# Decoding weights in a three-layer kernel: the sign bit through a parametric ReLU, and earlier decoding for the second layer

## The chip, the cores and the metric

The kernel runs on one core of a Trainium2 chip. The metric is the device time of one launch in microseconds, as the median of several runs. The core has a matrix engine (TensorE; PE in the profile, its weight loads PEld), VectorE (DVE), ScalarE (ACT), GpSimd (POOL) and SyncE (SP), whose queue issues all DMAs here. The engines work side by side and wait for each other through semaphores.

## The reference

Attention for 4 batches, 8 heads, 576 tokens of 64 values, half of the heads with a local mask and half with a strided one; then a gated layer and a softplus layer over the 2304 tokens. Cut to what matters:

```
attn = softmax(where(mask, q @ k.T / 8, -1e9)) @ v
x = attn as 2304 tokens x 512
xn = x / sqrt(mean(x * x) + 1e-6) * rms_g
g = xn @ w_gate;  x = (g / (1 + exp(-g))) * (xn @ w_val) @ w_out      # layer 1, 1536 wide
h = x @ w_in;  out = (max(h, 0) + log1p(exp(-|h|))) @ w_out2          # layer 2, 2048 wide
```

The weights arrive as 64-bit floating point numbers. The kernel reads their bits and makes 32-bit ones of them itself.

## The kernel before

All matrix products of the two layers are done in three matmuls of reduced 32-bit precision (L459): each operand is split into a high part (`ob`, `tb`, `win`, `wout`, `gh`, written by ACT) and a rest (written by DVE or POOL with a subtraction, L376 or L377 through `two`).

The 2304 tokens stand in five chunks of 512 (the last has 256). Layer 1 works on them in two passes. The first pass (chunks 0 and 1) runs while attention for the later batches is still computed, so PE has products of layer 1 (L459) between the small matmuls of attention (L604, L617, L706, L760). At its end the square sums of the last chunks are turned into factors (`stats`, L490 to L493), the chunks are scaled, and `combine` and `build` make the sums of a Strassen product (`tb`): the change of passes. The second pass (chunks 2 to 4) takes the 12 column blocks of layer 1 in a loop with the counter `s`; `quad` does the Strassen product of a block, and `chain1` silu and gate (L972, L974, L975). Then layer 2 goes over the chunks in the same two groups, with `chain2` for softplus.

`decode` (L384) makes one 128 x 512 tile of 32-bit weights. A 512 KB load brings the 64-bit words into one of two buffers `raw`. ACT scales the upper words, read as 32-bit numbers, by 2 to the power -112, which puts sign, exponent and mantissa where three left shifts bring them to their place (L392, into the tile `t`: `w`, `cvt` or `cvtx`). The three low bits of the mantissa come from the lower words into `cvu`: by ACT from a 16-bit view (L393) or by DVE with a shift to the right (L395). A left shift of `t` would push out the sign, so DVE first joins the sign to the low bits (L397) and then shifts `t` and joins both (L400). There are 74 decoded tiles: 42 of layer 1, of which six are decoded twice over the two passes (blocks 0 and 1), and 32 of layer 2. Layer 2's tiles are decoded ahead by `early2`, written back to memory (`w_kept`, L404) and fetched later (L407): 24 of them in the loop of the second pass, 8 in the first four steps of layer 2.

The order of all instructions is set by a planner (`Program`, `Trial`): it gets each instruction with an estimated length and its reads and writes, and lays out each engine's list by due times. Instructions with an `alt` may go to another engine: evictions of attention (`evict`, L291, L292 or L294) and the low bits to ACT or DVE, subtractions and sums (`two`) to DVE or POOL. A small change in `decode` thus moves instructions everywhere. Tables of activation functions are loaded by `table` (L304).

Of the kernel before, what the change touches and what calls it, by code (L numbers as in the profile page):

```python
# [10 lines left out]
F32 = mybir.dt.float32  # L11
F32R = mybir.dt.float32r
U16 = mybir.dt.uint16
U32 = mybir.dt.uint32
# [3 lines left out]
ALU = mybir.AluOpType  # L18
# [241 lines left out]
def attn_glu_softplus(  # L260
# [17 lines left out]
    def all_of(key):  # L278
        return (key, 0, 1 << 30)
# [20 lines left out]
    def dma(kb, fn, r, w):  # L300
        pr.add("SP", 650, fn, r, w, kb=kb)

    def table(name):
        pr.add("ACT", 1300, lambda: nc.scalar.preload_act_table_set(name), [], [all_of("table")])  # L304

    class Ring:
        def __init__(self, tiles, name, first=0):
# [76 lines left out]
    def decode(src, t, kt, keep):  # L384

        raw, kraw = raws.next()
        u, ku = cvu.next()
        words = raw.bitcast(U32).rearrange("p (n two) -> p n two", two=2)
        wlo, whi = words[:, :, 0], words[:, :, 1]
        quarters = raw.bitcast(U16).rearrange("p (n four) -> p n four", four=4)  # L390
        dma(340, lambda: nc.sync.dma_start(out=raw, in_=src), hold, [kraw])
        act(512, lambda: nc.scalar.activation(t, whi.bitcast(F32), AF.Copy, scale=2.0 ** -112), [kraw], [kt])  # L392
        pr.add("ACT", 180 + 512 / 0.98, lambda: nc.scalar.activation(  # L393
            u, quarters[:, :, 1], AF.Identity, bias=low, scale=2.0 ** -13), [kraw, all_of("eps")], [ku], alt=(68 + 512 / 1.5,
            lambda: nc.vector.tensor_scalar(out=u, in0=wlo, scalar1=29, scalar2=None,  # L395
                                            op0=ALU.logical_shift_right)))
        dve(560, lambda: nc.vector.scalar_tensor_tensor(  # L397
            out=u, in0=t.bitcast(U32), scalar=0x80000000, in1=u, op0=ALU.bitwise_and, op1=ALU.bitwise_or),
            [kt, ku], [ku])
        dve(560, lambda: nc.vector.scalar_tensor_tensor(  # L400
            out=t.bitcast(U32), in0=t.bitcast(U32), scalar=3, in1=u,
            op0=ALU.logical_shift_left, op1=ALU.bitwise_or), [kt, ku], [kt])
        if keep >= 3 * AGAIN:
            dma(170, lambda: nc.sync.dma_start(out=wk[keep], in_=t), [kt], [("wk", keep, keep + 1)])  # L404

# [683 lines left out]
    with tc.manual_schedule():  # L1089
# [141 lines left out]
        for s, f in enumerate([*range(AGAIN, W1N), *range(AGAIN)]):  # L1231
            prep1(f, 1)
            w = w_at(f, 1)
            c0, c1, c4 = SIDES[1]
            odd = []

            def gap(k):
                if 0 < k < 3:
                    odd.append(plain(w, k - 1, c4, o_banks))
                if k == 2:  # L1240
                    g[f, c4] = chain1(*odd, 256, True)
                if k and (s < W1N - 1 or len(todo) > 4):
                    drain(2 if f % 2 else 1)

            (gb0, vb0), (gb1, vb1) = quad(w, gap)
            g[f, c0] = chain1(gb0, vb0)
            g[f, c1] = chain1(gb1, vb1)
            for k in range(max(0, 3 * s - 6), min(3 * s - 3, 2 * W1N)):
                early2(k)
            drain(max(0, len(todo) - 6))  # L1250
            if f % 2:
                drain(len(todo))
                todo.extend(outs1(f, s == 1, (c0, c1, c4)))
        drain(len(todo))
        table("softplus")
        for side, (c0, c1, c4) in enumerate(SIDES):
# [2 lines left out]
            n2 = W2N // 2  # L1259
            for p in range(n2):  # L1260
                i = prep2(p, c4 is not None, "POOL" if p == 0 or side == 0 and p < 4 else "DVE")
                if side == 0 and p < 4:
                    early2(2 * W1N + 2 * p)
                    early2(2 * W1N + 2 * p + 1)
                def gap(k):
                    if c4 is not None and 0 < k < 3:
                        g[2 * p + k - 1, c4] = chain2(plain(i, k - 1, c4, o_banks), 256, True)
# [86 lines left out]
```

## Time and profile before

| | us |
|---|---|
| median of 3 runs | 892.98 |
| lowest, highest | 891.08, 894.34 |
| span of the profiled execution | 893.0 |
| PE busy in it | 877.7 |
| DVE busy | 716.4 |
| ACT busy | 509.1 |
| POOL busy | 66.2 |

The profiled execution's own time is its span, 893.0 us, from the first to the last instruction. PE's matmuls are pipelined: one of 512 columns is shown with about 0.39 us, and the next begins 0.23 us later, so a PE that is shown as busy may still lose a little. The clock granted to PE is shown as 1.00 of its full speed in nearly all of the span. Attention and the first pass of layer 1 reach to some 245 us, the change of passes to some 288, the second pass to some 515, layer 2 to the end.

### The profile page before, as it was taken

To read this page: it belongs to the slowest core of one execution; us is meant where nothing else is said; L and a number is where in the kernel's file an instruction comes from. 1 tells how busy PE (TensorE), PEld (TensorE's weight loads), DVE (VectorE), ACT (ScalarE), POOL (GpSimd) and SP (SyncE) were. 2 spreads that over 40 slices of the span, in tenths; PEclk is the share of its full clock that TensorE was granted. 3 is DMA by queue.
4 is the path that set the end of the run, shared out by engine and by line. 5 is a ranking of instruction groups with operands and counts; after the bars stand their busy time and mean duration, and the time that the engine had idled before them with its cause. 6 is when DMAs were issued, how large, how long until landed. Compare 5 with 4: busy or idle time off the path is not lost.

```text
span 893.0 us, 14103 instructions
## 1 busy us (share of the span) xinstructions
PE 877.7 (98%) x5372; PEld 726.9 (81%) x5372; DVE 716.4 (80%) x1316; ACT 509.1 (57%) x977; POOL 66.2 (7%) x60
## 2 busy tenths in 40 slices
PE   7999999999999999999999999999999999999998
PEld 6677877888877888888888888888888888888887
DVE  4999999997699986888889798877798466666645
ACT  3997766663454677564656478544474655434331
POOL 1010202110012001010100020000000000000000
PEclk8999999999999999999999999999999999999999
DMA  7755766532211256454542035311114011111003
GB/s 251 251 194 167 252 219 205 171 97 102 74 56 48 84 167 206 150 178 151 167 138 88 19 105 191 130 47 48 48 48 165 24 48 48 48 29 43 0 1 118
DMA packets 41140, 102.17 MB, mean 114 GB/s; under 512 B 4720, under 2 KB 5744, under 8 KB 41072
## 3 DMA queue, kind: packets, MB, share of 16 engines
q1 hardware_dynamic: 41072, 101.27, 35.1%
q8 instruction: 42, 0.69, 0.3%
q14 instruction: 26, 0.21, 0.1%
HBM read 80.28 MB, written 20.97 MB: 113 GB/s over the span
## 4 chain that ended last, share of the span: by engine, by line
PE 89%; DVE 6%; ACT 2%; DMA 1%; issue 1%; SPq 0%; DVEq 0%
PE bank L459 85%; PE bank L760 1%; DVE xs L1008 1%; PE bank L706 1%; PE bank L617 1%; DMA id_sb<-ident 1%; DVE tb L376 1%; DVE xs L376 1%; DVE gv L376 0%; PE bank L483 0%; ACT eb L664 0%; PE bank L604 0%; ACT eb L668 0%; DVE gv L492 0%; DVE w L376 0%
## 5 line engine op out<-in xcount | busy, mean ns | idle before, releaser
L459 PE MATMUL bank<-ob,win 128*128 128x512 f32 (+1 forms) x1560 | 438.8, 361 | 2.0 <-DVE xs L1008 0.7
L459 PEld LDWEIGHTS bank<-ob,win 128*128 128x128 f32 x1560 | 282.8, 188 | 55.8 <-issue 2.3
L459 PE MATMUL bank<-tb,win 128*128 128x512 f32 x672 | 232.5, 392 | 0.0
L459 PEld LDWEIGHTS bank<-tb,win 128*128 128x128 f32 x672 | 125.0, 188 | 22.9 <-ACT ssq L919 0.2
L1030 DVE TENSOR_TENSOR xs<-bank,xs 128x512 f32<-128x512 f32 (+1 forms) x127 | 87.1, 687 | 43.4 <-PE bank L459 41.7
L430 ACT ACTIVATE win<-w 128x512 fp32r<-128x512 f32 (+1 forms) x136 | 83.1, 615 | 49.2 <-PE bank L459 22.6
L459 PE MATMUL bank<-wout,ghx 128*128 128x512 f32 x304 | 99.9, 389 | 0.0
L459 PE MATMUL bank<-wout,gh 128*128 128x512 f32 (+1 forms) x276 | 90.3, 386 | 0.0
L376 DVE TENSOR_TENSOR win<-w,win 128x512 fp32r<-128x512 f32 (+1 forms) x121 | 82.3, 683 | 7.9 <-ACT win L430 5.2
L459 PE MATMUL bank<-ghx,wout 128*128 128x512 f32 x224 | 83.4, 392 | 0.0
L459 PE MATMUL bank<-gh,wout 128*128 128x512 f32 (+1 forms) x256 | 79.5, 352 | 1.0 <-DVE xs L1008 1.0
L1008 DVE TENSOR_TENSOR xs<-bank,xs 128x512 f32<-128x512 f32 (+1 forms) x100 | 62.6, 634 | 14.0 <-PE bank L459 12.6
L459 PEld LDWEIGHTS bank<-wout,ghx 128*128 128x128 f32 x304 | 56.9, 188 | 11.9
L459 PEld LDWEIGHTS bank<-wout,gh 128*128 128x128 f32 x276 | 51.3, 188 | 10.5
L459 PE MATMUL bank<-wout,glx 128*128 128x512 f32 x152 | 53.5, 389 | 0.0
L923 DVE TENSOR_TENSOR gv<-bank,gv 128x512 f32<-128x512 f32 x48 | 33.1, 690 | 24.4 <-PE bank L459 14.1
L459 PEld LDWEIGHTS bank<-gh,wout 128*128 128x128 f32 x256 | 45.2, 189 | 9.1 <-DVE xs L1008 1.9
L459 PEld LDWEIGHTS bank<-ghx,wout 128*128 128x128 f32 x224 | 42.0, 188 | 8.5
L459 PE MATMUL bank<-wout,gl 128*128 128x512 f32 (+1 forms) x138 | 48.0, 386 | 0.0
L376 DVE TENSOR_TENSOR w<-w 128x256 f32<-128x256 f32 x108 | 46.5, 430 | 0.9
L919 ACT ACTIVATE gv<-bank 128x512 f32<-128x512 f32 x48 | 28.6, 597 | 31.9 <-PE bank L459 31.4
L459 PE MATMUL bank<-glx,wout 128*128 128x512 f32 x112 | 43.3, 395 | 0.2 <-DVE glx L376 0.2
(162 smaller groups left out, 1276.4 us busy)
## 6 DMA issues: line engine op xcount, KB each, us to landing
raw<-w SPq DMA_DIRECT2D x74, 512.0 KB, 3.8
w<-w_kept SPq DMA_DIRECT2D x52, 256.0 KB, 2.6
qk<-qk SPq DMA_DIRECT2D x15, 608.0 KB, 6.7
w_kept<-cvtx SPq DMA_DIRECT2D x25, 256.0 KB, 2.8
cvt<-w_kept SPq DMA_DIRECT2D x25, 256.0 KB, 2.7
w_kept<-w SPq DMA_DIRECT2D x20, 256.0 KB, 2.7
w_kept<-cvt SPq DMA_DIRECT2D x17, 256.0 KB, 2.0
cvtx<-w_kept SPq DMA_DIRECT2D x17, 256.0 KB, 2.7
```

The source lines that it names most:

```text
L376: pr.add("DVE", 68 + n / 0.96, lambda: getattr(nc.vector, name)(o, x, y), r, w, alt=(110 + n * 2.3, lambda: getattr(nc.gpsimd, name)(o, x, ...
L430: act(n, lambda: nc.scalar.activation(h, t, AF.Copy), [kt], [reg(0, o + lo, o + hi)])
L459: lambda a=a, b=b, i=i, st=st, mv=mv: nc.tensor.matmul(o, lhsT=st[a], rhs=mv[b], start=(first and i == 0), stop=(last and i == m - 1), ski ...
L617: nc.tensor.matmul(sp[o, a * nk:(a + 1) * nk], lhsT=qt[r, c:c + 64], rhs=qt[r, QW + c:QW + c + nk], start=False, stop=True, skip_group_che ...
L706: pr.add("PE", 108, lambda a=a, a0=a0, tp=tp: nc.tensor.transpose(tp[:kp, a * 128:a * 128 + 128], pv[:, a0 + a, :], id_sb), [kpv, all_of(" ...
L760: pr.add("PE", 59 if loc else 36, lambda a=a, h=h, o=o, t=t: nc.tensor.matmul(xb[64 * h:64 * h + 64, a * nq:(a + 1) * nq], lhsT=vt[r0:r1, ...
L919: act(CH, lambda: nc.scalar.activation(o, y[0], AF.Copy), [y[1]], [ko])
L923: dve(CH, lambda: nc.vector.tensor_add(o[0], y[0], o[0]), [y[1], o[1]], [o[1]])
L1008: dve(n, lambda: nc.vector.tensor_add(x, pb, x), [kp, kx], [kx])
L1030: dve(n, lambda x=x, pb=pb: nc.vector.tensor_add(x, pb, x), [kp, kx], [kx])
```

## The change

In `decode` ACT's scaling becomes a parametric ReLU: positive numbers are scaled as before, negative ones are also multiplied by -2 to the power 32. Their result is positive and has bit 28 set, which the left shift by three brings to the sign's place. The instruction that joined the sign goes. What is left is one shift and one join. Where ACT makes the low bits, DVE shifts `t` and joins them as before. Where DVE takes that step (`shift`), it now shifts `t` into `cvu`, and the join reads the lower words of `raw` itself and shifts them to the right. Both forms of the second step now wait for the first; the join now also reads `raw`. The table for softplus waits for the last parametric ReLU (`slope`). In the loop of the second pass three tiles of layer 2 a step are decoded from the second step on, all 32 of them, and layer 2 decodes none.

```diff
-        pr.add("ACT", 1300, lambda: nc.scalar.preload_act_table_set(name), [], [all_of("table")])
+        pr.add("ACT", 1300, lambda: nc.scalar.preload_act_table_set(name), [], [all_of("table")] + [all_of("slope")] * (name == "softplus"))
...
+        ti = t.bitcast(U32)
         dma(340, lambda: nc.sync.dma_start(out=raw, in_=src), hold, [kraw])
-        act(512, lambda: nc.scalar.activation(t, whi.bitcast(F32), AF.Copy, scale=2.0 ** -112), [kraw], [kt])
+        act(512, lambda: nc.scalar.activation(t, whi.bitcast(F32), AF.Prelu, scale=2.0 ** -112, alpha=-2.0 ** 32),
+            [kraw, all_of("slope")], [kt])
+        shifted = []
+
+        def shift():
+            shifted.append(nc.vector.tensor_scalar(out=u, in0=ti, scalar1=3, scalar2=None, op0=ALU.logical_shift_left))
+
+        def join():
+            a, b, n, op = (wlo, u, 29, ALU.logical_shift_right) if shifted else (ti, u, 3, ALU.logical_shift_left)
+            nc.vector.scalar_tensor_tensor(out=ti, in0=a, scalar=n, in1=b, op0=op, op1=ALU.bitwise_or)
+
         pr.add("ACT", 180 + 512 / 0.98, lambda: nc.scalar.activation(
-            u, quarters[:, :, 1], AF.Identity, bias=low, scale=2.0 ** -13), [kraw, all_of("eps")], [ku], alt=(68 + 512 / 1.5,
-            lambda: nc.vector.tensor_scalar(out=u, in0=wlo, scalar1=29, scalar2=None,
-                                            op0=ALU.logical_shift_right)))
-        dve(560, lambda: nc.vector.scalar_tensor_tensor(
-            out=u, in0=t.bitcast(U32), scalar=0x80000000, in1=u, op0=ALU.bitwise_and, op1=ALU.bitwise_or),
-            [kt, ku], [ku])
-        dve(560, lambda: nc.vector.scalar_tensor_tensor(
-            out=t.bitcast(U32), in0=t.bitcast(U32), scalar=3, in1=u,
-            op0=ALU.logical_shift_left, op1=ALU.bitwise_or), [kt, ku], [kt])
+            u, quarters[:, :, 1], AF.Identity, bias=low, scale=2.0 ** -13), [kraw, kt, all_of("eps")], [ku],
+            alt=(68 + 512 / 1.92, shift))
+        dve(560, join, [kraw, kt, ku], [kt])
...
-            for k in range(max(0, 3 * s - 6), min(3 * s - 3, 2 * W1N)):
+            for k in range(max(0, 3 * s - 3), min(3 * s, 2 * W2N)):
                 early2(k)
...
-                if side == 0 and p < 4:
-                    early2(2 * W1N + 2 * p)
-                    early2(2 * W1N + 2 * p + 1)
```

The code behind `decode` stands five lines lower in the changed kernel (L459 becomes L464). The planner's lists change in many places. Three of them follow.

PE in the front, the last part before layer 1 and attention run without gaps. `bank_72` and `bank_71` with `ob,win` are the 12 and 12 products of block 1 with chunk 0; `L706` (`L711` after) are transposes of attention, `L760` (`L765`) its products with v. Before:

```order
L706 MATMUL bank_73<-id_sb,eb_120 96x128 x3
L706 MATMUL bank_74<-id_sb,eb_120 96x128
L459 MATMUL bank_72<-ob,win_90 128x512 x9
L760 MATMUL bank_75<-pt_124,xs 64x64 x6
L760 MATMUL bank_75<-pt_125,xs 64x64 x2
L459 MATMUL bank_72<-ob,win_90 128x512 x3
L706 MATMUL bank_73<-id_sb,pp_123 128x128 x3
L706 MATMUL bank_74<-id_sb,pp_123 128x128 x3
L459 MATMUL bank_71<-ob,win_90 128x512 x2
L760 MATMUL bank_76<-pt_126,vb_114 64x54 x3
```

After:

```order
L464 MATMUL bank_72<-ob,win_90 128x512 x3
L711 MATMUL bank_73<-id_sb,eb_120 96x128 x3
L711 MATMUL bank_74<-id_sb,eb_120 96x128
L464 MATMUL bank_72<-ob,win_90 128x512 x9
L765 MATMUL bank_75<-pt_124,xs 64x64 x6
L765 MATMUL bank_75<-pt_125,xs 64x64 x2
L464 MATMUL bank_71<-ob,win_90 128x512 x9
L711 MATMUL bank_73<-id_sb,pp_123 128x128 x3
L711 MATMUL bank_74<-id_sb,pp_123 128x128 x3
L464 MATMUL bank_71<-ob,win_90 128x512 x3
L765 MATMUL bank_76<-pt_126,vb_114 64x54 x3
```

All 24 products now stand ahead of that `L765`, 14 did before; the other ten stood behind it and its neighbours.

DVE in the same place, up to the first instruction of the gate (`L972`, `L977` after). `mz` and `pp` belong to attention's softmax. Before:

```order
L397 SCALAR_TENSOR_TENSOR cvu_82<-w_83,cvu_82 128x512
L679 TENSOR_SCALAR mz_133<-mz_133 128x5
L376 TENSOR_TENSOR pp_123<-eb_121,mz_132 128x6x54
L680 RECIPROCAL mz_133<-mz_133 128x5
L400 SCALAR_TENSOR_TENSOR w_83<-w_83,cvu_82 128x512
L376 TENSOR_TENSOR pp_123<-eb_117,mz_133 128x5x54
L493 SCALAR_TENSOR_TENSOR ssq<-gv_84,ssq 128x512
L395 TENSOR_SCALAR cvu_82<-raw_80 128x512
L972 TENSOR_TENSOR gv_85<-bank_77,ssq 128x512
```

After:

```order
L402 SCALAR_TENSOR_TENSOR cvtx<-raw_80,cvu_82 128x512
L376 TENSOR_TENSOR pp_123<-eb_121,mz_132 128x6x54
L683 TENSOR_REDUCE mz_133<-eb_117 128x5
L291 COPY xs<-bank_75 128x128
L684 TENSOR_SCALAR mz_133<-mz_133 128x5
L292 TENSOR_SCALAR xs<-bank_75,rg_sb 128x128
L685 RECIPROCAL mz_133<-mz_133 128x5
L498 SCALAR_TENSOR_TENSOR ssq<-gv_84,ssq 128x512
L376 TENSOR_TENSOR pp_123<-eb_117,mz_133 128x5x54
L977 TENSOR_TENSOR gv_85<-bank_77,ssq 128x512
```

The tile `w` of block 1 is now joined further ahead, the next tile (`cvtx`) stands where its join stood, and evictions (`xs<-bank`) stand between. From the same instruction at 24.91 us to the first `L975` (`L980`), DVE has 91 instructions before and 96 after.

POOL in the change of passes. Before:

```order
L377 TENSOR_TENSOR xs<-xs,ssq_b 128x512
L377 TENSOR_TENSOR win_90<-w_83,win_90 128x512
L377 TENSOR_TENSOR ob<-xs,ob 128x512
L377 TENSOR_TENSOR w_83<-w_83 128x256
L377 TENSOR_TENSOR win_90<-w_83,win_90 128x512
L377 TENSOR_TENSOR ob<-xs,ob 128x256
L377 TENSOR_TENSOR tb<-xs,tb 128x512
L377 TENSOR_TENSOR xs<-xs,ssq 128x512
```

After:

```order
L377 TENSOR_TENSOR xs<-xs 128x512
L377 TENSOR_TENSOR wout_99<-cvtx,wout_99 128x512
L377 TENSOR_TENSOR win_90<-w_83,win_90 128x512
L377 TENSOR_TENSOR ob<-xs,ob 128x512
L377 TENSOR_TENSOR tb<-xs,tb 128x512
L377 TENSOR_TENSOR xs<-xs,ssq 128x512
```

Eight become six; in the same place (from the first `ssq_b` of the statistics to the first sum of the Strassen product) DVE's 68 become 70.

## Rows read from the trace of the kernel before

**Rows 1.** The page's first part: busy us, share of span, instructions.

```profile
PE 877.7 (98%) x5372; PEld 726.9 (81%) x5372; DVE 716.4 (80%) x1316; ACT 509.1 (57%) x977; POOL 66.2 (7%) x60
```

**Rows 2.** The chain in order of time: start us, us, what.

```profile
284.96 105.70 PE bank L459 x552
...
525.82 362.90 PE bank L459 x1687
```

**Rows 3.** Stretches: length; busy PE, PEld, DVE, ACT, POOL; PE clock; DMA share; GB/s.

```profile
24.91:60.37 35.46, 31.85 (x466) 23.39 (x467) 33.58 (x92) 32.74 (x109) 4.25 (x6) 1.00 0.73 235
60.15:243.12 182.97, 182.48 (x1416) 146.54 (x1417) 160.14 (x306) 115.95 (x207) 23.28 (x21) 1.00 0.50 159
246.30:288.49 42.19, 40.26 (x178) 32.12 (x177) 42.01 (x69) 21.86 (x38) 10.43 (x8) 1.00 0.16 49
285.00:511.00 226.00, 225.97 (x1177) 193.27 (x1178) 194.30 (x348) 137.93 (x243) 15.77 (x13) 1.00 0.41 133
```

**Rows 4.** Groups by line: busy us, mean ns; idle before, and what ended it.

```profile
L393 ACT ACTIVATE cvu<-raw,low 128x512 uint32<-128x512 uint16 x44 | 33.6, 764 | 15.0 <-DVE cvtx L400 8.1 <-DVE w L400 4.6 <-DVE cvt L400 1.5
...
L397 DVE SCALAR_TENSOR_TENSOR cvu<-w,cvu 128x512 uint32<-128x512 uint32 x28 | 19.2, 685 | 3.3 <-ACT cvu L393 1.8 <-ACT w L392 1.4
...
L392 ACT ACTIVATE w<-raw 128x512 f32<-128x512 f32 x28 | 18.5, 672 | 7.1 <-DMA raw<-w 3.4 <-DVE mz L632 2.9 <-DVE win L376 0.6
```

**Rows 5.** Stretches, L397 alone: length, DVE busy (count), clock, DMA share, GB/s.

```profile
25.00:62.00 37.00, 4.09 (x6) 1.00 0.73 233
62.00:245.00 183.00, 19.86 (x29) 1.00 0.50 158
285.00:525.00 240.00, 21.79 (x30) 1.00 0.38 126
525.00:893.00 368.00, 5.51 (x8) 1.00 0.21 69
```

**Rows 6.** DVE in order of time, front: start us, us, instruction, idle before.

```profile
21.48 0.49 DVE L291 COPY pt<-bank 128x324 f32<-128x324 f32 x1
21.89 0.42 DVE L291 COPY xs<-bank 128x256 f32<-128x256 f32 x1
...
50.41 0.35 DVE L292 TENSOR_SCALAR xs<-bank,rg_sb 128x72 f32<-128x72 f32 x1 [0.33 <-ACT xs L294]
...
57.50 0.42 DVE L395 TENSOR_SCALAR cvu<-raw 128x512 uint32<-128x512 uint32 x1
57.84 0.68 DVE L972 TENSOR_TENSOR gv<-bank,ssq 128x512 f32<-128x512 f32 x1
...
59.77 0.68 DVE L397 SCALAR_TENSOR_TENSOR cvu<-cvtx,cvu 128x512 uint32<-128x512 uint32 x1
60.37 0.69 DVE L975 TENSOR_TENSOR gv<-bank,gv 128x512 f32<-128x512 f32 x1
```

**Rows 7.** The page's DMA issues: count, size of one, us from issue to landing.

```profile
raw<-w SPq DMA_DIRECT2D x74, 512.0 KB, 3.8
```

**Rows 8.** PE in order of time, end of the front.

```profile
60.08 2.79 PE L459 MATMUL bank<-ob,win 128*128 128x512 f32 x11
62.86 0.73 PE L459 MATMUL bank<-gh,wout 128*128 128x512 f32 x2
```

**Rows 9.** POOL and DVE in order of time, change of passes.

```profile
249.08 1.41 POOL L377 TENSOR_TENSOR xs<-xs,ssq_b 128x512 f32<-128x512 f32 x1 [56.48 <-DVE ssq_b L493]
...
249.85 2.89 DVE L376 TENSOR_TENSOR xs<-xs,ssq_b 128x512 f32<-128x512 f32 x2
```

**Rows 10.** Waits of PE, 236 to 290 us: total us, times, longest.

```profile
PE bank L459 <- DVE xs L1008: 1.7, 3, 0.7
```

**Rows 11.** Groups by line: the loads of activation tables.

```profile
L304 ACT ACT_TABLE_LOAD x13 | 16.7, 1283 | 0.9 <-PEq L1342 0.7
```

## The prediction

> **What bounds the kernel now.** I read the page's busy times first, then the chain of work in order of time, then the busy time by stretch, then the waits of the stretches in which PE is not full. PE is busy for 98% of the span, DVE for 80%, ACT for 57% [rows 1]. The chain says what that means: from 284.96 us on it is PE for 105.70 us, and from 525.82 us for 362.90 us, with nothing between PE's instructions [rows 2]. By stretch PE is busy for 182.48 of 182.97 us in the second part of attention and 225.97 of 226.00 us in the second pass of layer 1 [rows 3]. There an instruction less on DVE shortens nothing. Two stretches are left. In the front, 24.91 to 60.37 us, PE is busy for only 31.85 of 35.46 us, while DVE is at 33.58 and ACT at 32.74 us: both feed PE late. In the change of passes, 246.30 to 288.49 us, PE has 40.26 of 42.19 us and DVE 42.01 [rows 3]. The whole visible idle time is 3.6 us in the one and 1.9 us in the other, and the change has to earn its gain there.
>
> **Part 1, one DVE instruction a tile less.** The joining of the sign (L397) goes for all 74 tiles: 6, 29, 30 and 8 in the four stretches shown, one more between them [rows 5]. It lasts 685 ns [rows 4], but the next DVE instruction starts 0.60 us after it (59.77 to 60.37) [rows 6], so DVE gives back 74 x 0.60 = 44 us. Of these, 29 x 0.60 = 17 us (part of attention) and 38 x 0.60 = 23 us (layers 1 and 2) lie beside a full PE and are worth nothing. Six, 3.6 us, lie in the front.
>
> **Part 2, what replaces it.** On ACT a Copy with a scale becomes a parametric ReLU with a scale. The trace has no such instruction. Below, its bound is the Copy's 672 ns; above, the Identity with a pointer bias, 764 ns [rows 4]. I take the Copy, since both slopes are constants in the instruction; the upper end would cost ACT 6 x 0.09 = 0.5 us in the front. The three low bits still come from ACT (46 tiles, 44 before) or, in 28 tiles, from DVE as a shift of one source; the shift before it kept DVE for 0.34 us (57.50 to 57.84) [rows 6] and the new one does the same on unstrided data, so I cost that edit at nothing. New are two waits. The low bits now wait for the first pass over the tile. On ACT that is the instruction just ahead in its own queue; on DVE it delays what is queued behind by at most the Copy's 0.67 us, where the order has put other work between. And in the DVE form the raw words are held until the join, some 0.34 + 0.60 us longer plus what stands between, about 1.5 us. What covers this is that two raw buffers alternate and a load lands in 3.8 us [rows 7], while tiles come 183 / 29 = 6.3 to 240 / 30 = 8 us apart [rows 5]; if that cover were gone a tile would come 1.5 us late.
>
> **Part 3, the eight tiles that move.** They leave layer 2 (526 us on, 8 of the L397 [rows 5]) for the second pass of layer 1. With them go eight loads and eight stores on SP's queue, eight to sixteen ACT instructions and eight to sixteen on DVE, ahead of other work there. DVE loses 30 x 0.60 = 18 us in that pass and takes at most 8 x (0.60 + 0.34) = 7.5 us; ACT rises from 137.9 by at most 8 x (0.67 + 0.76) = 11.4 us of 226; the DMA engines are at 0.41 [rows 3]. So PE hides it on both sides, and I cost it at nothing. The softplus table now waits for the last of them, decoded in the last round of a loop in which PE is full. If that cover were gone, softplus would start later by one load and one decode, 3.8 + 0.67 + 0.94 = 5.4 us.
>
> **Part 4, the new order in the front.** The planner spends the 3.6 us. Up to the first gate product (L975, at 60.37 us before), DVE has 96 instructions instead of 91: six sign joins less, one final join more, one split of `win` less (it goes to POOL), and in their place eleven evictions of attention from ACT, one `ob` and one `pp`. At the rows' pitch (0.41 us for the largest eviction, 21.48 to 21.89 [rows 6]; 0.20 to 0.41 for the rest) that is -3.6 + 0.6 - 0.6 + 4.25 = +0.65 us. ACT's own list to the first silu comes out even. PE, in the order, does all 24 products of the first half ahead of the place where it did 14 before. Ten matmuls at 0.25 us (60.08 to 62.86 us for 11 [rows 8]) look like 2.5 us won. They aren't: before, these ten and one more ran from 60.08 to 62.86 us and covered the wait for `gh`, which PE read at once when it came [rows 8]. After the change PE reaches the same `gh` with the same 49 products behind it, and the end is set by when DVE and ACT deliver `gh`. DVE idles for 35.46 - 33.58 = 1.9 us on the way there [rows 3]; the moved evictions take some of those waits with them. Ends: +0.65 us if none goes, 0.65 - 1.9 = -1.25 us if all does. I take half of it, -0.3 us, and -0.2 us for the mask matmuls that PE has done by then: **-0.5 us**.
>
> **Part 5, the change of passes.** Here DVE sets the pace: 68 instructions, which at 0.60 us (0.33 for half tiles) are 37.6 us, took 42.19 us. The rest, 4.6 us, goes where POOL works on the same data paths: two DVE instructions that should start 0.60 us apart took 2.89 us at 249.85, while POOL ran [rows 9, 6]. POOL has eight instructions there, so 0.57 us each. After the change DVE has 70 (38.0 us, +0.4) since the last decode moves ahead of the stretch and others come in, and POOL has six: -1.1 us. The stretch gets 0.7 us shorter, and PE waits there for DVE's L1008 [rows 10], so PE gets it: **-0.7 us**. Ends: +0.4 us if POOL's two cost nothing, -1.9 us if all of PE's idle time goes.
>
> The page "SBUF — State Buffer" of the Trainium skill (section "SBUF: two separate sides") says that DVE with two SBUF inputs and a GpSimd instruction that reads SBUF exclude each other for a whole instruction. The 2.89 us agrees with it. By that rule two POOL instructions less would be worth up to their own 1.41 us each, 2.8 us instead of 1.1, and this stretch would fall to the end of -1.9 us; that is in the second case below.
>
> **Sum.** The profiled span is 893.0 us, and the median of the three runs 892.98, so nothing is to be added. 893.0 - 0.5 - 0.7 = **891.8 us**.
>
> **The rivals.** *Both stalls go.* DVE's waits in the front vanish with the moved evictions (-1.25 - 0.2) and PE's idle time in the change of passes too (-1.9): 893.0 - 3.35 = 889.6 us. For it: DVE is full in both stretches [rows 3], and the freed instruction is on the chain there. Against: the order shows that the planner has filled DVE up again. *Nothing moves.* What DVE saves is taken by what ACT and POOL hand to it, and the places at which PE waits shift: 893.0 us. For it: +0.65 and +0.4 us are nearly the whole of what the order gives and takes.
>
> *Slower: the gate chain comes late in the front.* Eleven evictions now stand in DVE's queue, each waiting for PE's transposes or products, and the chain to `gh` stands behind them. One such wait before an eviction's partner was 0.33 us [rows 6]. At 0.25 us each, a little less, that is 2.75 us, with the 0.65 us of work 3.4 us. The ten matmuls that could have filled the gap are already done, so PE stands idle for all of it: 893.0 + 3.4 - 0.7 = 895.7 us. It decides from the point where the new waits exceed the old 1.9 us. Against it: ACT, which had these evictions, was as full.
>
> *The new function brings table loads.* A table load lasts 1283 ns and there are 13 [rows 11]; the order of the changed kernel has 13 too. If the activation were in neither of the two sets used in attention and layer 1, each of 74 tiles would need two, 74 x 2 x 1.28 = 190 us on ACT, and the time would be far over 1000 us. The page "ScalarE: Activation LUTs" of the Trainium skill (section "Table sets: the hidden batching unit") says that cheap functions stand in every set, and that a back-end pass adds a load where one is missing. No row here shows which sets hold the new one.
>
> **How the numbers follow.** Forecast (890.6 to 893) 0.42, both stalls gone (889.6, down to 888) 0.28, nothing 0.16, slower (894.3 to 896) 0.12, table loads 0.02. A measurement of this kernel can tell about 0.3%, 2.7 us, from no change: the bounds are 890.3 and 895.7. Below 890.3 lies most of the second case and a little of the first: 0.30. Above 895.7 the upper part of the late gate chain and the table loads: 0.09. Within: 0.61. The range runs from 888.6, which leaves out 0.09 below, to 894.9, which leaves out 0.11 above.
>
> **What would show it.** The parametric ReLU near 670 ns; no sign join; 13 table loads. PE's first read of `gh` in layer 1 between 61.4 and 63.5 us. The change of passes near 41.5 us, with POOL's rows there fewer and DVE's long instructions gone from it. From there to the end the same length as before, within 1 us: the second pass and layer 2 full on PE, DVE less busy in both. I am wrong if PE waits inside layer 2 or at its start (part 3), if PE waits over 1 us for `gh` (part 4), or if the pass of attention between 62 and 243 us gets shorter by more than the front gives it, which would mean that PE's full rows hide waits.

## The result and the profile after

The changed kernel takes 901.81 us (median of 4 executions, 898.89 to 902.95) beside 893.48 us for the kernel before: a ratio of 1.0083, 95% interval 1.0060 to 1.0106. It is slower by 8 us, and in a second series by 7 (901.08 beside 893.89). Its profiled execution is the fastest of the four: 898.89 us for a span of 896.7, so 2.2 us lie outside the span. The four spans are 896.7, 898.5, 900.8 and 900.8 us, with mean granted clocks of 0.996, 0.994, 0.990 and 0.991.

The page's first part, as in [rows 1]:

```profile
PE 878.3 (98%) x5372; PEld 726.8 (81%) x5372; DVE 684.0 (76%) x1265; ACT 503.0 (56%) x959; POOL 67.9 (8%) x55
```

DVE is busy for 32 us less than before, ACT for 6 us less, and PE, which has the same 5372 matmuls, is not done sooner. The groups of the decoding (busy us, mean ns; idle time before and what ended it), to be read beside [rows 4] and [rows 11]:

```profile
L404 ACT ACTIVATE cvu<-raw,low 128x512 uint32<-128x512 uint16 x46 | 34.8, 756 | 9.3 <-DVE w L402 5.9 <-DVE cvtx L402 2.7 <-DVE cvt L402 0.8
L393 ACT ACTIVATE w<-raw 128x512 f32<-128x512 f32 x28 | 18.7, 670 | 3.9 <-DVE win L376 2.6 <-DMA raw<-w 1.3
...
L304 ACT ACT_TABLE_LOAD x13 | 16.7, 1283 | 0.9 <-PEq L1344 0.7
...
L402 DVE SCALAR_TENSOR_TENSOR cvtx<-cvtx,cvu 128x512 uint32<-128x512 uint32 x12 | 11.4, 954 | 0.4 <-ACT cvu L404 0.2
L402 DVE SCALAR_TENSOR_TENSOR cvt<-cvt,cvu 128x512 uint32<-128x512 uint32 x16 | 10.9, 684 | 1.2 <-ACT cvu L404 1.2
```

The parametric ReLU takes the Copy's time (670 ns), and no table load came in. The join takes 684 ns where nothing disturbs it and 954 ns as the mean of 12 others. Where PE stands idle is seen by stretch (columns as in [rows 3]):

```profile
60.00:120.00 60.00, 57.65 (x495) 44.63 (x495) 51.10 (x105) 46.59 (x86) 10.99 (x10) 1.00 0.67 208
120.00:180.00 60.00, 58.00 (x498) 45.86 (x498) 48.85 (x88) 32.73 (x57) 10.13 (x8) 1.00 0.54 167
180.00:246.00 66.00, 66.00 (x419) 53.88 (x412) 46.50 (x89) 31.28 (x54) 4.36 (x4) 1.00 0.29 94
246.00:290.00 44.00, 41.28 (x180) 33.30 (x180) 43.70 (x73) 23.32 (x41) 15.05 (x6) 1.00 0.20 63
290.00:520.00 230.00, 228.90 (x1195) 195.02 (x1194) 188.60 (x338) 143.41 (x253) 12.60 (x10) 1.00 0.48 154
520.00:893.00 373.00, 373.00 (x1746) 312.11 (x1745) 258.21 (x438) 183.00 (x336) 6.59 (x3) 1.00 0.17 53
```

In the same stretches PE was busy before for 60.00, 59.51, 66.00, 42.07 and 229.97 us. It is idle for 2.4, 1.5, 0.8 and 1.1 us more in four stretches, two of which had been full, while DVE is *less* busy in all four (56.28, 57.28, 43.82 and 198.19 before). The waits of PE name the releaser (total us, times, longest); 60 to 245 us and then 245 to 530 us:

```profile
PE bank L464 <- DVE gvx L980: 1.4, 1, 1.4
PE bank L464 <- DVE gv L977: 1.1, 2, 0.9
PE bank L609 <- DVE gv L980: 1.0, 1, 1.0
PE bank L464 <- DVE gv L980: 0.5, 1, 0.5
...
PE bank L464 <- DVE xs L1013: 2.7, 2, 2.0
PE bank L464 <- DVE gv L928: 1.1, 2, 0.6
```

Before, these two lists came to 0.5 and 1.9 us; now they come to 4.4 and 3.8. L977 and L980 are the two products of the gate (`chain1`), L928 a sum of `quad`, L1013 the eviction of layer 1's products. Two places show how a DVE that has less to do comes later. At 163 us, DVE, then POOL, then PE, in order of time:

```profile
156.54 0.67 DVE L977 TENSOR_TENSOR gvx<-bank,ssq 128x512 f32<-128x512 f32 x1
...
158.34 0.68 DVE L376 TENSOR_TENSOR win<-w,win 128x512 fp32r<-128x512 f32 x1
158.94 1.78 DVE L376 TENSOR_TENSOR wout<-cvtx,wout 128x512 fp32r<-128x512 f32 x1
160.65 1.78 DVE L376 TENSOR_TENSOR xs<-xs,ssq_b 128x512 f32<-128x512 f32 x1
162.35 0.54 DVE L291 COPY pt<-bank 96x384 f32<-96x384 f32 x1
162.82 0.67 DVE L980 TENSOR_TENSOR gvx<-bank,gvx 128x512 f32<-128x512 f32 x1
...
158.54 3.33 POOL L377 TENSOR_TENSOR xs<-xs,ssq_b 128x512 f32<-128x512 f32 x2 [3.68 <-issue]
...
163.54 0.50 PE L464 MATMUL bank<-ob,win 128*128 128x512 f32 x1 [1.38 <-DVE gvx L980]
```

Between the two products of this gate, L977 and L980, DVE's queue has six instructions of other work. Two of them take 1.78 us instead of 0.68 while POOL works, 2.2 us more together; PE waits 1.38 us for L980. The same, on a smaller scale, happens ahead of two other waits for the gate. At 82 us a DVE instruction on five numbers a partition (its group's median is 158 ns) takes 1.25 us beside POOL; at 156 us a join (L402, at 153.64) takes 1.78 us:

```profile
79.48 1.61 POOL L377 TENSOR_TENSOR win<-w,win 128x512 fp32r<-128x512 f32 x1 [20.97 <-ACT win L435]
...
79.87 1.25 DVE L684 TENSOR_SCALAR mz<-mz 128x5 f32<-128x5 f32 x1
...
82.38 1.62 PE L464 MATMUL bank<-ob,win 128*128 128x512 f32 x6 [0.89 <-DVE gv L977]
...
153.12 1.74 POOL L377 TENSOR_TENSOR wout<-cvt,wout 128x512 fp32r<-128x512 f32 x1 [7.44 <-DVE xs L1013]
...
156.07 1.19 PE L464 MATMUL bank<-ob,win 128*128 128x512 f32 x4 [0.51 <-DVE gv L980]
```

The second place is the change of passes, POOL, DVE and PE:

```profile
255.96 3.64 POOL L377 TENSOR_TENSOR wout<-cvtx,wout 128x512 fp32r<-128x512 f32 x1
259.56 4.85 POOL L377 TENSOR_TENSOR win<-w,win 128x512 fp32r<-128x512 f32 x1
265.12 1.59 POOL L377 TENSOR_TENSOR ob<-xs,ob 128x512 fp32r<-128x512 f32 x1 [0.71 <-ACT ob L365]
266.68 1.73 POOL L377 TENSOR_TENSOR tb<-xs,tb 128x512 fp32r<-128x512 f32 x1
...
260.16 0.68 DVE L376 TENSOR_TENSOR tb<-gv,tb 128x512 fp32r<-128x512 f32 x1
260.76 0.68 DVE L376 TENSOR_TENSOR win<-w,win 128x512 fp32r<-128x512 f32 x1
...
265.49 1.78 DVE L376 TENSOR_TENSOR ob<-xs,ob 128x512 fp32r<-128x512 f32 x1
267.18 1.77 DVE L376 TENSOR_TENSOR tb<-gv,tb 128x512 fp32r<-128x512 f32 x1
...
269.48 0.68 DVE L1013 TENSOR_TENSOR xs<-bank,xs 128x512 f32<-128x512 f32 x1
...
270.21 0.50 PE L464 MATMUL bank<-gh,wout 128*128 128x512 f32 x1 [2.03 <-DVE xs L1013]
```

Two subtractions that POOL does in 1.3 us elsewhere take 8.5 us here; POOL's next two then fall beside DVE's, DVE is late with L1013 by 2.2 us, and PE waits 2.03 us.

### The profile page after: what moved, and what is told of

The parts are those of the page before. It is cut to its first block, busy times and chain, and to the rows that moved or that the text cites. A ratio compares the mean times of both kernels' runs of the same rounds, so it can differ in the third digit from the quotient of the medians.

```text
span 896.7 us, 14021 instructions
## 1 busy us (share of the span) xinstructions
PE 878.3 (98%) x5372; PEld 726.8 (81%) x5372; DVE 684.0 (76%) x1265; ACT 503.0 (56%) x959; POOL 67.9 (8%) x55
## 4 chain that ended last, share of the span: by engine, by line
PE 88%; DVE 7%; ACT 3%; DMA 1%; issue 1%; SPq 0%; DVEq 0%
PE bank L464 83%; PE bank L765 1%; PE bank L711 1%; PE bank L622 1%; DVE xs L1013 1%; DMA id_sb<-ident 1%; DVE xs L376 1%; PE bank L488 1%; DVE cvtx L402 1%; DVE gv L376 0%; DVE tb L376 0%; ACT eb L669 0%; DVE gv L977 0%; ACT ob L371 0%; PE bank L609 0%
## 5 line engine op out<-in xcount | busy, mean ns | idle before, releaser
L464 PE MATMUL bank<-ob,win 128*128 128x512 f32 (+1 forms) x1560 | 435.5, 361 | 3.8 <-DVE gvx L980 1.4
L464 PEld LDWEIGHTS bank<-ob,win 128*128 128x128 f32 x1560 | 283.5, 188 | 57.7 <-issue 3.7
L464 PE MATMUL bank<-tb,win 128*128 128x512 f32 x672 | 232.4, 392 | 1.1 <-DVE gv L928 1.1
L464 PEld LDWEIGHTS bank<-tb,win 128*128 128x128 f32 x672 | 125.3, 188 | 24.5 <-DVE gv L928 1.9
L464 PE MATMUL bank<-wout,ghx 128*128 128x512 f32 x304 | 99.9, 390 | 0.0
L376 DVE TENSOR_TENSOR win<-w,win 128x512 fp32r<-128x512 f32 (+1 forms) x124 | 82.6, 668 | 20.3 <-ACT win L435 15.1
L464 PE MATMUL bank<-wout,gh 128*128 128x512 f32 (+1 forms) x276 | 90.5, 387 | 0.0
L464 PE MATMUL bank<-ghx,wout 128*128 128x512 f32 x224 | 83.4, 393 | 0.0
L464 PE MATMUL bank<-gh,wout 128*128 128x512 f32 (+1 forms) x256 | 79.3, 350 | 2.1 <-DVE xs L1013 2.0
L1013 DVE TENSOR_TENSOR xs<-bank,xs 128x512 f32<-128x512 f32 (+1 forms) x100 | 62.6, 632 | 18.1 <-PE bank L464 16.5
L464 PEld LDWEIGHTS bank<-wout,ghx 128*128 128x128 f32 x304 | 56.9, 188 | 11.7
L464 PEld LDWEIGHTS bank<-wout,gh 128*128 128x128 f32 x276 | 51.5, 188 | 10.5
L464 PEld LDWEIGHTS bank<-gh,wout 128*128 128x128 f32 x256 | 45.4, 189 | 9.7 <-DVE xs L1013 2.5
L464 PE MATMUL bank<-wout,glx 128*128 128x512 f32 x152 | 53.2, 389 | 0.0
L464 PEld LDWEIGHTS bank<-ghx,wout 128*128 128x128 f32 x224 | 42.0, 188 | 8.6 <-issue 0.2
L928 DVE TENSOR_TENSOR gv<-bank,gv 128x512 f32<-128x512 f32 x48 | 33.0, 687 | 20.4 <-ACT gv L924 10.4
L464 PE MATMUL bank<-wout,gl 128*128 128x512 f32 (+1 forms) x138 | 48.1, 386 | 0.0
L464 PE MATMUL bank<-glx,wout 128*128 128x512 f32 x112 | 43.0, 394 | 0.0
```

The costliest lines, as they stand in the source:

```text
L376: pr.add("DVE", 68 + n / 0.96, lambda: getattr(nc.vector, name)(o, x, y), r, w, alt=(110 + n * 2.3, lambda: getattr(nc.gpsimd, name)(o, x, ...
L464: lambda a=a, b=b, i=i, st=st, mv=mv: nc.tensor.matmul(o, lhsT=st[a], rhs=mv[b], start=(first and i == 0), stop=(last and i == m - 1), ski ...
L928: dve(CH, lambda: nc.vector.tensor_add(o[0], y[0], o[0]), [y[1], o[1]], [o[1]])
L1013: dve(n, lambda: nc.vector.tensor_add(x, pb, x), [kp, kx], [kx])
```

## The experiments

Theories: *form* (an instruction or wait of the new decoding costs the time on the chip), *place* (the eight moved tiles), *order* (what costs is the new order of all engines that the planner makes when it is given other nodes). All medians stand beside 893.6 to 894.1 us for before in the same series. PE's waits are the sums of the waits in the profile, in us (e8 has the waits of the changed kernel, but one of 1.0 us ends at 59.4 us, ahead of the column).

| kernel | median us | ratio to before (95%) | PE waits 60 to 245 | 245 to 530 |
|---|---|---|---|---|
| before | 893.5 | | 0.5 | 1.9 |
| changed, again (e8) | 901.1 | 1.0074 (1.0059, 1.0089) | 3.4 | 3.8 |
| e1: order of before, no sign join | 894.1 | 0.9997 (0.9982, 1.0011) | 1.3 | 1.9 |
| e3: eight tiles moved only | 893.7 | 0.9994 (0.9982, 1.0006) | 0.5 | 1.7 |
| e2: decoding only, planned anew | 899.5 | 1.0061 (1.0048, 1.0073) | 4.4 | 4.4 |
| e9: order of the changed one, no new waits | 900.1 | 1.0064 (1.0042, 1.0086) | 4.4 | 3.8 |
| e4: POOL's work to DVE | 899.4 | 1.0058 (1.0046, 1.0070) | 3.7 | 1.3 |
| e5: no new waits, planned anew | 891.9 | 0.9974 (0.9963, 0.9984) | 0.8 | 0.0 |
| e6: before, another order | 902.6 | 1.0094 (1.0079, 1.0109) | 4.4 | 1.9 |
| e12: before, a third order | 896.4 | 1.0026 (1.0014, 1.0037) | 2.0 | 1.9 |
| e7: changed, another order | 897.9 | 1.0041 (1.0029, 1.0053) | 3.1 | 2.5 |
| e10: changed, a third order | 896.3 | 1.0029 (1.0015, 1.0043) | 0.4 | 4.2 |
| e11: e5 in another order | 897.2 | 1.0034 (1.0017, 1.0051) | 0.9 | 2.3 |
| e15: two subtractions to DVE | 898.0 | 1.0043 (1.0029, 1.0058) | 4.4 | 2.5 |
| e14: first part before, second changed | 895.8 | 1.0019 (1.0009, 1.0030) | 1.4 | 3.8 |
| e16: first part changed, second e5's way | 895.9 | 1.0022 (1.0009, 1.0034) | 4.4 | 1.2 |
| e13: first part before, second e5's way | 890.4 | 0.9965 (0.9954, 0.9976) | 0.5 | 0.3 |

Over these 17 kernels the median grows by 1.2 us for each us that PE waits behind 60 us (correlation 0.87; e6 fits worst, 3.7 us over the line, and it also has 5.7 us of waits from 25 to 60 us, where before has 3.3, one of them, 2.0 us, in both counts, and a clock of 0.990 to 0.992 in its four executions, where before mostly has 0.994 to 0.998). Behind 530 us none has more than 0.3.

**The instructions in the old order, and the two halves of the change apart.** e1 leaves the planner's nodes, lengths and order of before and empties the slot of the sign join (shortened; the eight tiles decoded in layer 2 keep the old form):

```diff
-            t, whi.bitcast(F32), AF.Copy, scale=2.0 ** -112), [kraw], [kt])
+            t, whi.bitcast(F32), AF.Prelu, scale=2.0 ** -112, alpha=-2.0 ** 32), [kraw], [kt])
...
-        dve(560, lambda: nc.vector.scalar_tensor_tensor(out=u, ..., scalar=0x80000000, ...), [kt, ku], [ku])
+        dve(560, lambda: None, [kt, ku], [ku])
```

> The kernel before with its planner's nodes, lengths and order untouched; only what is emitted changes: the scaling is the parametric ReLU and the slot of the sign join stays empty, for 66 tiles (the eight tiles of layer 2 keep the old decoding, since they stand behind the softplus table). The shift of DVE stays the old one of the lower words. Theory 'order' (the loss of the changed kernel comes from the order that the planner makes anew, not from the instructions): no loss, 891.5 to 893.5 us, so 0 to 2 us faster than before: at most 3.6 us of DVE in the front and part of PE's 1.9 us in the change of passes. Rival 'form' (the new first instruction or the missing join itself makes PE late, for example by moving the collisions of DVE with POOL): slower than before by several us, 896 to 902 us.

> The new decoding as in the changed kernel, planned anew, but the eight tiles of layer 2 stay in layer 2 with the old decoding. Theory 'order': planned anew, so it loses like the changed kernel or by another amount of the same size, 895 to 903 us, at other places. Rival 'place' (the eight tiles moved into the second pass cost the time): 891 to 893.5 us.

> The old decoding (Copy, sign join), but all 32 tiles of layer 2 decoded in the second pass as in the changed kernel, planned anew. Rival 'place': the loss is here, 898 to 903 us, and PE waits lie in the second pass. Theory 'order': the first planning part (up to 245 us) is the same as before, so only the second part can lose: 892 to 897 us.

e1: 894.1 us, the time of before, though DVE is busy for 676.9 us instead of 716.4. Forty us of DVE are worth nothing, and the new function costs nothing. e3: 893.7, so moving the eight tiles costs nothing. e2: 899.5, with the waits of the changed kernel at the same places (its lists of the first part are the same). The loss comes with planning the new decoding, not with running it.

**The waits on the chip.** e9 keeps every engine's list of the changed kernel and takes the new waits away:

```diff
         def shift():
-            shifted.append(nc.vector.tensor_scalar(out=u, in0=ti, scalar1=3, scalar2=None, op0=ALU.logical_shift_left))
+            nc.vector.tensor_scalar(out=u, in0=wlo, scalar1=29, scalar2=None, op0=ALU.logical_shift_right)
 
         def join():
-            a, b, n, op = (wlo, u, 29, ALU.logical_shift_right) if shifted else (ti, u, 3, ALU.logical_shift_left)
+            a, b, n, op = ti, u, 3, ALU.logical_shift_left
```

> Every engine's list in the order of the changed kernel, line for line, but the two new waits are not there on the chip: where DVE makes the low bits it shifts the lower words (28 tiles), and the join reads the tile and the low bits, not the raw words. If the waits themselves cost the time on the chip (DVE behind the first instruction, the raw buffer held until the join): 892 to 896 us. If they cost it only through the order that the planner builds around them: no gain, 899.5 to 902 us.

900.1 us: with or without the waits the order costs 6 to 7 us. *Form* is out, on both sides (e1, e9).

**Is it this order, or any new one?** e5 also takes the two waits out of the planner's nodes; e6, e7, e10, e11 and e12 change numbers of the planner alone (shortened, several edits in one):

```diff
-            u, quarters[:, :, 1], AF.Identity, ...), [kraw, kt, all_of("eps")], [ku],
-            alt=(68 + 512 / 1.92, shift))
-        dve(560, join, [kraw, kt, ku], [kt])
+            u, quarters[:, :, 1], AF.Identity, ...), [kraw, all_of("eps")], [ku],
+            alt=(68 + 512 / 1.5, shift))               # e5; shift and join as in e9
+        dve(560, join, [kt, ku], [kt])
...
-SLACK = 10                                             # e6 on before, e11 on e5
+SLACK = 12
...
-TURNS, KEEP, SWITCH, LEAVE = 8, 0.5, 125, 4000         # e7 on the changed kernel
+TURNS, KEEP, SWITCH, LEAVE = 16, 0.7, 125, 4000
...
-BESIDE = 900                                           # e10 (1100) and e12 (1000, on before)
+BESIDE = 1100
```

> The changed kernel itself, once more, beside the others of this series. In its first profile PE had lost 3.7 us more than before between 25 and 246 us and 0.9 us more behind that, while the medians lay 8 us apart. If the loss is only what PE waits for in its new order, the median comes out at 897 to 898 us. If some executions also get a lower granted clock, it stays at 899 to 902 us, with single times from 898 to 903.

> The changed kernel without its two new waits: the parametric ReLU and one join a tile, but the low bits read the lower words and wait for nothing but the load, on ACT as on DVE (the shift to the right of before), and the join reads the tile and the low bits alone. All 32 tiles in the second pass. Planned anew. Theory 'waits' (the low bits behind the first instruction, and the raw words held until the join, make the order worse): 891 to 894 us. Theory 'any new plan costs' (the order of before is a lucky one of many, and each edit draws a new one): anything from 892 to 902, most likely 897.

> The kernel before, not one instruction changed: only the planner's allowance for each DVE and ACT instruction is 12 ns instead of 10, which draws another order. The planner's own estimate rises from 878.8 to 882.1 us, 3.3 us in the first part. Theory 'any new plan costs': slower by 2 to 8 us, 896 to 902. Theory 'waits': the order matters little as long as the instructions are the same, 892 to 895 us.

> The changed kernel, instructions and waits unchanged, with another order: the planner makes 16 tries instead of 8 and keeps 0.7 of the old due times from try to try instead of 0.5. Its own estimate for the first part falls from 232.6 to 231.3 us (before: 231.7). Theory 'any new plan costs' (the loss is the draw): it differs from the changed kernel, 892 to 897 us. Theory 'waits' (the new decoding is bad in every order): 898 to 902 us.

> The changed kernel's instructions and waits in a third order (POOL is offered work only when 1100 ns instead of 900 of it stand before DVE; the planner's estimate of the first part is 231.6 us, 232.6 in the changed kernel). Theory 'any new plan costs': somewhere between 892 and 903. Theory 'waits': 897 us or more in every order.

> The version without the two new waits (891.9 us) in another order (12 ns instead of 10 allowed for each DVE and ACT instruction; estimate of the first part 232.1 us instead of 231.5). Theory 'waits': 890 to 895 us in this order too. Theory 'any new plan costs': 895 to 902, as the kernel before went from 893.9 to 902.6 with the same edit.

> The kernel before in a third order (POOL is offered work when 1000 ns instead of 900 stand before DVE; estimate of the first part 233.6 us instead of 231.7). Theory 'any new plan costs': 896 to 902 us. Theory 'waits': 892 to 896.

The kernel before, without one instruction changed, takes 893.5, 896.4 or 902.6 us by its order; the changed one 901.1, 897.9 or 896.3; e5 891.9 or 897.2. So the draw is 5 to 9 us wide. Against the expectations: e11 and e12 came out as "any new plan costs" said, e6 too but 0.6 us above its range; e7 lies between its two ranges; e5 is faster, as "waits" said, so a new order need not cost; and e10 shows that it need not be worse than 897 us with the new waits. The order of before is the best of its three, that of the change the worst of its three; whether the new waits make orders worse on the average can't be told from three draws each. e6's largest waits are 2.7 us at 32 us, for nothing that the profile shows, and 2.0 us at 60 us, for a subtraction of attention on DVE; its granted clock is 0.76 from 30 to 35 us and 0.50 from 60 to 65 us. e8 stayed at 901.1 us, as expected if some executions also get a lower clock; its six have 0.991 to 0.996.

**POOL beside DVE.** e4 keeps the order of the changed kernel and issues POOL's flexible work on DVE in the same place; e15 does so for two instructions, those of 3.64 and 4.85 us (both in short):

```diff
-               alt=(110 + n * 2.3, lambda: getattr(nc.gpsimd, name)(o, x, y)))
+               alt=(110 + n * 2.3, lambda: getattr(nc.vector, name)(o, x, y)))    # e4: all; e15: two of them
```

> The changed kernel in its own order, but the subtractions and sums that the planner gave to POOL are issued by DVE in the same place of the order (0.69 us instead of 1.3 us each, some 45 of them). Theory 'collisions' (the loss comes from DVE's and POOL's instructions that hold each other up on the shared paths): the long DVE instructions of 1.6 to 1.8 us vanish, PE's waits at 161, 268, 390 and 430 us with them, 896 to 898.5 us median instead of 901.8. Rival (the loss is in the order of the work itself, waits on late evictions and joins): no gain or slower by up to 3 us, 901 to 905 us.

> The changed kernel in its own order, but two subtractions of the change of passes (of wout and win, for which POOL took 3.64 and 4.85 us from 255.96 us on) are issued by DVE in the same place, 0.6 us each. If they are what makes PE wait 2.0 us at 267 us and lets the clock drop behind it in some executions: 897.5 to 899.5 us, and no PE wait over 1 us between 260 and 275 us. If DVE was the bound there and POOL only its relief: 901 to 902.5 us.

e4 gains 1.7 us on the changed kernel (899.4 beside 901.1), less than expected and inside the spread of the changed kernel's own executions (897.3 to 903.0). The waits at 82, 156 and 164 us, 2.8 us together, shrink to one of 0.4. The two in the second pass, for L928, 0.55 us each, are gone; in the changed kernel a join (L402) of 1.75 us stands just ahead of L928 both times (at 389.03 and 428.70 us), beside a subtraction of POOL (from 388.94 and 428.61 us on). So POOL beside DVE makes most of these waits. But DVE has some 45 instructions more, other waits come in, the one at 61 us grows from 1.0 to 1.4 us, and in its profile the clock falls twice (0.50 from 50 to 52 us, 0.79 from 60 to 65). In e15 the wait of 2.03 us in the change of passes becomes two of 0.7:

```profile
PE bank L470 <- DVE gv L983: 0.7, 1, 0.7
PE bank L470 <- DVE xs L1019: 0.7, 1, 0.7
```

It gains some 3 us, more than the 1.3 us of waits; the clocks, 0.994 to 1.000 beside 0.991 to 0.996 in e8, go the same way. POOL was no relief there; it was the cause.

**Where in the program.** The first part (to 246 us) and the second are planned one after the other. e13, e14 and e16 join the parts, by choosing the nodes of `decode` before and behind the first planning (before it stand the nodes of e1 in e13 and e14, those of the changed kernel in e16; behind it those of the changed kernel in e14, those of e5 in e13 and e16):

```diff
+        if not later:
...
+        else:
...
             pr.emit()
+            later.append(1)
```

> First part in the order of before with the sign join's slot empty, second part planned anew with the parametric ReLU, one join and no new waits, all 32 tiles in the second pass. If the gain of the version without the new waits (891.9 us, beside 893.9 for before) lies in its change of passes, where PE did not wait at all: 890 to 892 us. If its first part brought the gain: 893 to 894.5.

> First part in the order of before with the sign join's slot empty, second part planned anew with the changed kernel's instructions and both new waits. If the loss lies in the first part: 892 to 895 us. If the second part holds half of it or more: 896 to 899.

> First part that of the changed kernel, line for line, second part planned anew without the two new waits. If the loss lies in the first part: 897 to 901 us. If the second part holds half of it or more: 892 to 896.

e14 lies between its two ranges, and e16 in the range that was to speak for the second part. That range was set as if e5's second part took the time of before's; e13 shows that it is 3.5 us faster (893.9 to 890.4), so e16 is read against e13. With the second part of e5, the changed first part costs 895.9 - 890.4 = 5.5 us; with its own second part, 901.1 - 895.8 = 5.3 us. The second part costs 895.8 - 893.9 = 1.9 us. (5.3 and 1.9 add up to the whole loss by the way they are formed; what is measured twice is the first part.) e13 is faster than both kernels, 890.4 us; in its change of passes PE is never idle:

```profile
255.00:260.00 5.00, 5.00 (x24) 4.15 (x23) 5.00 (x10) 4.16 (x8) 0.00 (x0) 1.00 0.00 0
260.00:265.00 5.00, 5.00 (x24) 4.14 (x23) 5.00 (x10) 1.72 (x4) 2.26 (x2) 1.00 0.19 54
265.00:270.00 5.00, 5.00 (x24) 4.14 (x23) 4.80 (x10) 2.27 (x5) 0.42 (x1) 1.00 0.01 3
```

Its DVE is as full as that of the changed kernel there; POOL (the last count, ahead of the clock) has little, and none of its instructions there takes over 1.7 us.

How far a profile lies behind e13's at the same amount of issued matmul columns (512 columns counted as the 0.227 us at which PE begins them; us):

| profile, at e13's | 25 us | 246 us | 288 us | 525 us |
|---|---|---|---|---|
| before | 2.0 | 1.9 | 5.3 | 5.5 |
| changed | 1.2 | 4.9 | 8.2 | 9.5 |
| e9, same order | 1.9 | 6.9 | 11.8 | 12.9 |
| e16, same first part | 1.2 | 6.0 | 8.0 | 7.3 |
| e14, same second part | -1.8 | -1.1 | 3.8 | 5.0 |

The changed kernel loses 3.7 us in the first part (before loses nothing, -0.1); e9 and e16 lose 5.0 and 4.8 with the same lists. In the change of passes it loses 3.3 us, as before does (3.4), but e9 and e14 lose 4.9 with that list. The difference is the granted clock, below. From 288 to 525 us, the second pass, the changed kernel loses 1.3 us and before 0.2.

## Why the prediction was wrong

- **Part 1** was right: e1 shows that DVE's 40 us are worth nothing. The 3.6 us of them in the front brought nothing either.
- **Part 2** was right in its terms: 670 ns, 13 table loads, and the waits cost nothing on the chip (e9).
- **Part 3** was right as an edit (e3). PE has no wait in layer 2.
- **Part 4** was right for the front itself, by these lines:

```profile
60.78 0.35 PE L609 MATMUL bank<-mask 64*64 64x384 bf16 x2 [1.02 <-DVE gv L980]
...
61.52 0.62 PE L464 MATMUL bank<-gh,wout 128*128 128x512 f32 x2
```

PE's first read of `gh` came at 61.52 us instead of 62.86 [rows 8], with the same matmuls behind it and six mask matmuls more. At 25 us the changed profile was already 0.8 us ahead (table above), so the front became 0.5 us shorter, as forecast; e2 and e8 give 0.5 us too. The 1.02 us for the gate product just ahead, of the size that I had named as a sign of being wrong, are inside this balance. The same chain then made PE wait at 82, 156 and 164 us. My slower rival had the mechanism (a DVE chain that stands behind more work, PE with nothing left to fill in) but set it in the front, with 2.75 us; it cost behind it, and L977 and L980 make up 4.0 of the 4.4 us of waits from 60 to 245 us.
- **Part 5** failed. I counted POOL's instructions, eight to six, at 0.57 us each. POOL's time there went from 10.4 to 15.1 us. How an instruction meets DVE's sets its price, not the number of them. Instead of -0.7 us the stretch changed by nothing, or by +1.5 us where the clock fell (e9, e14).
- **The step that failed most** is "So PE hides it on both sides, and I cost it at nothing" (part 3), which I used for all that the new order moves beside a full PE. The runs show a cost there instead. The first part's loss of 3.8 us against before is -0.5 us up to the first `gh` and +4.3 us behind it, in rows that had been full; the second pass, also full before, loses 1.1 us more, which is as long as PE now waits there for a sum of `quad` (L928). By the medians the new order of the first part costs 5.3 to 5.5 us (e14, e16). A full row says that in *this* order all feeders come in time. It is true of an edit in that order (e1, e3) and says nothing of another. I had costed a few places of the new order and treated the rest as hidden. I named attention getting shorter between 62 and 243 us as a sign against me; that it could get longer, as it did, I did not.
- **The missing rival** was that a new order is a draw of 5 to 9 us' width, and that before's is a good draw. With it, slower would have been the likelier side: two of two other orders of before are slower by over 0.25%.
- Two smaller slips. The span leaves out about 2 us (895.27 for 893.5 in e1), so it is not the execution's own time, as I had said, and the profile of before belongs to an execution a little above the median. It doesn't move the forecast. And part 4's list adds up to 98 instructions, not 96: two of the eleven evictions stand ahead of 24.91 us, where the count begins, so 0.4 to 0.8 us of the 4.25 us do not belong to it.

What stays open: by the lags of its profile the change loses 3.8 us in the first part, by the medians 5.4, and 1.0 against 1.9 in the second. The clock drops below are of that size, and the times on record bear them out in sum: the ten executions of the changed kernel have a mean span of 898.7 us at a mean clock of 0.9930, the 29 of before 892.2 us at 0.9958. Among executions of one and the same kernel, over all runs, the span is 0.56 us longer for each 0.001 of clock less. By that, an estimate, 1.6 of the 6.5 us go with the clock, and 4.9 are left beside the 4.8 us of the lags. Where the clock falls in the slower executions isn't known; I have no profile of them. That POOL and DVE in each other's way cause the waits is shown for the change of passes (e15) and, with other waits coming in, for those in the second pass and most of those at 82, 156 and 164 us (e4). It isn't the cause at 61 us, where DVE's instructions keep their length and the wait stays in e4.

## What to carry to other kernels

Where a planner sets the order, an edit is two things: the instructions, and a new draw of the order. Measure them apart: emit the new instructions in the old order, and plan the old instructions anew; here the first changed the time by 0.0%, the second by 0.3 to 0.9%. A full PE hides extra work of a feeder only in the order in which it is seen full; after a change, sum PE's waits by releaser before anything else. And parts that are planned apart can be drawn apart: the first part in the order of before with the second part of e5 (e13) was 0.35% faster than the kernel before.

## What the chip showed that was not expected

**POOL gives way for long.** From 255.96 to 263.77 us DVE's instructions with two sources kept their pace of 0.60 us (260.16 to 260.76 in the fence above) while two subtractions of POOL stretched from 1.3 to 3.64 and 4.85 us; a little later DVE's took 1.78 instead of 0.68. The page "SBUF — State Buffer" of the Trainium skill (section "SBUF: two separate sides") says that whichever of the two starts first holds the shared ports for its whole instruction. DVE's extra 1.1 us agree with that. POOL's 3.64 and 4.85 us show the other side: with a queue of such instructions on DVE, several of DVE's went ahead while one of POOL's was under way.

**A wait of one or two us can cost its length again.** In all six profiles with the changed kernel's first part PE waits 1.1 us at about 49 us. In four of them the granted clock stays at 1.00. In e9 (50 to 54 us) and e16 it falls, almost to the lower level (0.5, 1.2 GHz) in the mean of some 4 us. Stretches of e9, the clock behind POOL's column:

```profile
48.00:50.00 2.00, 1.00 (x33) 0.85 (x32) 2.00 (x6) 1.64 (x8) 0.18 (x1) 1.00 0.86 292
50.00:52.00 2.00, 1.93 (x36) 1.82 (x38) 1.57 (x7) 2.00 (x12) 0.58 (x2) 0.61 0.93 287
52.00:54.00 2.00, 2.00 (x16) 1.50 (x13) 1.29 (x4) 1.25 (x3) 1.28 (x1) 0.54 0.95 268
...
270.00:275.00 5.00, 2.98 (x9) 2.17 (x8) 5.00 (x9) 1.57 (x3) 0.45 (x1) 0.73 0.00 0
275.00:280.00 5.00, 5.00 (x22) 4.11 (x21) 3.34 (x7) 0.87 (x2) 0.00 (x0) 0.93 0.01 3
```

The same after the 2.0 us wait of the change of passes: 0.73 and 0.93 in e9, 0.68 in e14, and 1.00 in the four other profiles with that wait. By the table of lags the two drops cost 1.3 and 1.6 us. That is most of the 3.4 us by which e9's span is longer than the changed kernel's with the same lists, and it fits the changed kernel's other executions, with clocks of 0.990 to 0.994. It isn't special to the change: in all 18 profiles the clock falls ten times behind 25 us, in e1 and e6 too, each time within 1.3 us of the end of a PE wait of 1.0 to 2.7 us; 32 of 42 such waits have no fall. That the wait brings the fall is argued from this order in time; no run tests it.

**The start varies.** Before and e3 have the same lists in the first part, and at 25 us one profile is 3.5 us behind the other, with granted clocks of 0.66 and 0.66 against 0.66 and 1.00 from 10 to 15 and from 15 to 20 us. Single profiles are compared from 25 us on.
